# A fused delta-rule and two-MoE kernel: the early groups in an order made step by step from durations, groups 0 and 1 in halves

## Chip, cores and metric

The kernel runs on one core of a Trainium2 chip. The metric is the device time of one execution in microseconds (us), the median of several runs; less is better. Engines are named as in the profile: PE is TensorE, DVE is VectorE, ACT is ScalarE, POOL is GpSimd, SP is SyncE, whose queue issues all loads and stores.

## The reference

A delta-rule attention (4 batches, 8 heads, 768 positions, head size 48) feeds a gated layer of 1536 channels, and that feeds an ELU layer of 2048 channels. Inputs of the attention are float32, the weights of both layers float64.

```python
k_n = k / (np.linalg.norm(k, axis=-1, keepdims=True) + 1e-06)
for t in range(S):
    y[:, :, t] = einsum('bhd,bhde->bhe', q[:, :, t], state)
    v_old = einsum('bhde,bhd->bhe', state, k_n[:, :, t])
    state = state + beta_t * einsum('bhd,bhe->bhde', k_n[:, :, t], v[:, :, t] - v_old)
x = y.transpose(0, 2, 1, 3).reshape(3072, 384)
g = x @ w_gate
x = (g / (1 + exp(-g)) * (x @ w_val)) @ w_out          # first layer, d_ff 1536
h = x @ w_in
out = where(h > 0, h, exp(minimum(h, 0)) - 1) @ w_out2 # second layer, d_ff 2048
```

## The kernel before

**Groups.** The 3072 tokens are 12 groups of 256: two batches by 128 positions each. A group's attention is in the chunked form of the delta rule and has two parts. The first part needs no other group: the norm of k (`norm`, `nkn`), transposes of q and k (`trans`, L207), Gram products (`gram`, L217, masked on DVE at L220), and the inverse of a triangular matrix, done on DVE in some 116 small multiplies and adds between transposes (`inversion`, L234 to L270), copied at L200 to `zt`. The second part is serial from group to group: the x-step (L288: the inverse by v and k, which stand side by side in `R`), four g-steps (L304, copied on ACT at L308, added on DVE at L309), four state rounds `chain` (L322, added at L326), `yall` (L335, copied at L341), and `xtr` (L351), which transposes y into the pair xh, xl (a rounded value on ACT, the remainder by a subtraction on DVE, L356 and L359).

**First layer.** Each group has 12 slices of 128 channels. For each, a gate/value product `gv_pe` (18 matmuls, L478) goes into one of two PSUM tiles gv0, gv1; silu on ACT (L504), multiply on DVE (L505), cast and subtract to hb; and an output product `out1` (9 matmuls, L521) adds into the PSUM tile `acc`, two products behind (`LAG`). After the twelfth slice `acc` is copied by ACT (L528) to `y` and stored to the DRAM tile `x2d`.

**Weights.** They come as the bits of float64 in 18 tiles w0 to w17 (three for two slices) and are decoded by six pieces each: "low" (ACT, L400), "sign" (ACT, L435; in the second layer "and", DVE, L420), "abs" (ACT, L407), "or" (DVE, L425), "cast" (ACT, L440), "sub" (DVE, L444). The weights of the second layer take the places of those of the first as they come free. The second layer (`h2`, `out2`) works on 512 tokens at a time; `load_x2` reads x back from `x2d` before it (L545).

**Order.** A scheduler of the language puts instructions on the engines in the order in which they are written, unless ready earlier; `inorder` forbids it to move those on DVE, ACT and POOL. The start is written out in order by hand: `merge` takes lists of (weight, step) and mixes them in proportion to the weights. Group 0's products stand in one merged, ordered list with the decoding slots and the attention of group 1; from group 1 on the attention of group g+1 is merged with the products of group g (`ATT`), and from g above 1 the last part of the inversion of g+2 is carried into the next period (`XTR`). SP's loads stand where the code issues them: v of group 0 behind w0 and w1.

## Time and profile before

| | |
|---|---|
| median of 3 runs | 1242.88 us (1241.53 to 1244.37) |
| the profiled execution | 1240.22 us, of which the span of the trace is 1238.5 us |
| PE busy | 1148.1 us, 93% of the span |
| DVE busy | 789.2 us, 64% |
| ACT busy | 626.9 us, 51% |
| POOL busy | 67.4 us, 5% |
| chain that ended last | PE 79%, DVE 12%, ACT 5%, issue 2%, DMA 1% |

The shares are over the whole span. The page's row of 40 slices (31 us each) shows PE at 2, 4, 7, 4 tenths in the first four slices and at 9 from the fifth to the last; DVE and ACT are busiest in the first four. The granted clock of PE is under full in slices 2 to 7 and full after. So a reader looks at the first slices apart from the rest.

### The profile page before, as it was taken

The page shows a single profiled execution, that of the slowest core. Times are in us where ns is not written, and L with a number is a line of the kernel's source. Part 1 is how long each engine was busy: PE and PEld are TensorE (multiplying, and loading weights), DVE is VectorE, ACT ScalarE, POOL GpSimd, SP SyncE. Part 2 cuts the span into 40 slices and gives each one's busy share as a digit, 9 for nine tenths or more (in the row PEclk, how much of TensorE's full clock was granted, in tenths as well). Part 3 has the DMA queues.
Part 4 walks back from the last instruction along what each step waited for, and adds up shares of the span by engine and source line. Part 5 has one row for each costly group of instructions (what it writes and reads, how often), then busy time and mean ns, then how long its engine had stood idle before and what let it go on. Part 6 is the DMA issues. An engine that isn't in the chain of part 4 may idle for free.

```text
span 1238.5 us, 31273 instructions
## 1 busy us (share of the span) xinstructions
PE 1148.1 (93%) x13086; PEld 1069.0 (86%) x13086; DVE 789.2 (64%) x2731; ACT 626.9 (51%) x1189; POOL 67.4 (5%) x76
## 2 busy tenths in 40 slices
PE   2474998999999999999999999999999999999998
PEld 2464898889899899999989999989899899899897
DVE  6779648768585849586858664549844545454443
ACT  6597634352526262635344433559744545454443
POOL 4000101010101010100000000000000000000000
PEclk9866799799999999999999999999999999999999
DMA  9730020212121110303030100580000101010000
GB/s 291 197 78 1 14 38 4 41 28 28 27 28 39 16 40 15 53 2 53 2 53 2 29 15 2 181 296 26 21 31 1 52 1 51 1 35 1 26 1 26
DMA packets 106813, 57.15 MB, mean 46 GB/s; under 512 B 76944, under 2 KB 101520, under 8 KB 106672
## 3 DMA queue, kind: packets, MB, share of 16 engines
q1 hardware_dynamic: 106672, 55.16, 17.6%
q8 instruction: 102, 1.67, 0.6%
q14 instruction: 39, 0.32, 0.1%
HBM read 45.71 MB, written 9.44 MB: 45 GB/s over the span
## 4 chain that ended last, share of the span: by engine, by line
PE 79%; DVE 12%; ACT 5%; issue 2%; DMA 1%; POOL 1%; SPq 0%; ACTq 0%; DVEq 0%
PE gv L478 21%; PE acc L521 10%; PE acc L573 8%; PE at L573 8%; PE gv L556 8%; PE at L556 8%; PE at L304 5%; PE at L288 3%; DVE z L262 3%; DVE ain L255 3%; PE at L322 3%; PE at L207 2%; PE at L335 1%; PE at L217 1%; DVE tb L505 1%
## 5 line engine op out<-in xcount | busy, mean ns | idle before, releaser
L478 PE MATMUL gv<-xh,w 128*128 128x256 f32 x1728 | 292.9, 292 | 27.8 <-DVE tb L505 23.4
L478 PEld LDWEIGHTS gv<-xh,w 128*128 128x128 f32 x1728 | 243.6, 196 | 34.7 <-DVE tb L505 25.0
L521 PE MATMUL acc<-hb,w 128*128 128x256 f32 x1296 | 187.4, 290 | 2.0 <-ACT y L528 1.6
L521 PEld LDWEIGHTS acc<-hb,w 128*128 128x128 f32 x1296 | 167.7, 194 | 5.8 <-ACT y L528 1.8
L478 PE MATMUL gv<-xl,w 128*128 128x256 f32 x864 | 155.3, 289 | 0.0
L504 ACT ACTIVATE tb<-gv 128x256 f32<-128x256 f32 x144 | 55.2, 384 | 160.7 <-PE gv L478 158.9
L356 ACT CAST hb<-tb 128x256 fp32r<-128x256 f32 x144 | 58.4, 406 | 149.8 <-DVE tb L505 149.6
L505 DVE TENSOR_TENSOR tb<-gv,tb 128x256 f32<-128x256 f32 x144 | 60.5, 421 | 114.9 <-ACT tb L504 114.2
L478 PEld LDWEIGHTS gv<-xl,w 128*128 128x128 f32 x864 | 127.8, 196 | 0.8 <-DVE xl L359 0.2
L255 DVE TENSOR_TENSOR ain<-z,ain 128x60 f32<-128x60 f32 (+32 forms) x696 | 120.3, 205 | 1.6
L262 DVE TENSOR_TENSOR z<-z,ain 128x60 f32<-128x60 f32 (+32 forms) x696 | 119.7, 210 | 1.4
L563 DVE SCALAR_TENSOR_TENSOR hb<-at,hb 128x512 f32<-128x512 f32 x48 | 33.2, 692 | 84.5 <-ACT hb L562 84.5
L563 DVE SCALAR_TENSOR_TENSOR hb<-gv,hb 128x512 f32<-128x512 f32 x48 | 33.2, 691 | 80.6 <-ACT hb L562 80.6
L359 DVE TENSOR_TENSOR hb<-tb,hb 128x256 fp32r<-128x256 f32 x144 | 60.6, 421 | 28.7 <-ACT hb L356 28.3
L304 PE MATMUL at<-gr,R 32*96 32x80 f32 x1472 | 73.0, 270 | 3.3 <-DVE lc L309 2.5
L304 PEld LDWEIGHTS at<-gr,R 32*96 32x96 f32 x1472 | 61.0, 173 | 14.7 <-DVE lc L309 3.0
L560 ACT ACTIVATE hb<-at 128x512 f32<-128x512 f32 x48 | 28.6, 596 | 85.3 <-PE at L556 85.3
L560 ACT ACTIVATE hb<-gv 128x512 f32<-128x512 f32 x48 | 28.6, 596 | 85.0 <-PE gv L556 85.0
L562 ACT ACTIVATE hb<-hb,neg 128x512 f32<-128x512 f32 x96 | 69.4, 723 | 2.8
L288 PE MATMUL at<-R,zt 64*64 64x96 f32 x768 | 42.9, 264 | 29.9 <-ACT zt L200 29.8
L288 PEld LDWEIGHTS at<-R,zt 64*64 64x64 f32 x768 | 39.5, 147 | 32.9 <-ACT zt L200 31.7
L561 ACT ACTIVATE hb<-hb 128x512 f32<-128x512 f32 x96 | 60.7, 632 | 2.6
(193 smaller groups left out, 2120.6 us busy)
## 6 DMA issues: line engine op xcount, KB each, us to landing
w<-in_moe_w_out_dram SPq DMA_DIRECT2D x28, 384.0 KB, 6.0
w<-in_moe_w_in_dram SPq DMA_DIRECT2D x16, 384.0 KB, 5.2
kp<-in_k_dram SPq DMA_DIRECT2D x12, 384.0 KB, 5.5
qp<-in_q_dram SPq DMA_DIRECT2D x12, 384.0 KB, 4.4
w<-in_moe_w_gate_dram SPq DMA_DIRECT2D x12, 384.0 KB, 8.6
w<-in_moe_w_val_dram SPq DMA_DIRECT2D x12, 384.0 KB, 8.6
R<-in_v_dram SPq DMA_DIRECT2D x24, 192.0 KB, 2.9
x2d<-y SPq DMA_DIRECT2D x12, 256.0 KB, 2.1
```

The source lines that it names most:

```text
L255: V.tensor_tensor(out=t, in0=z[:, l:l + 1, x:y].to_broadcast([128, l, y - x]), in1=an[:, l, 0:l].unsqueeze(2).to_broadcast([128, l, y - x] ...
L262: V.tensor_tensor(out=z[:, 0:l, x:y], in0=z[:, 0:l, x:y], in1=t, op=ALU.add)
L288: nc.tensor.matmul(p[r:r + 64, j], lhsT=zt[r:r + 64, 4 * n + j, :], rhs=R[r:r + 64, 4 * n + j, :], start=True, stop=True, skip_group_check ...
L304: nc.tensor.matmul(ps_[c][0:96, s * 80:s * 80 + 80], lhsT=R[t, u, :], rhs=gr[t, u, 0:80], start=True, stop=True, skip_group_check=True)
L478: nc.tensor.matmul(dst, lhsT=wt[:, a_, kk * 128:(kk + 1) * 128], rhs=xx[:, kk, :], start=(n == 0), stop=(n == 3 * KD - 1))
L505: V.tensor_tensor(out=s, in0=p[:, TB:2 * TB], in1=s, op=ALU.mult)
L521: nc.tensor.matmul(o, lhsT=w[:, a_, d * 128:(d + 1) * 128], rhs=hh[:, b_, :], start=(f == 0 and n == 0 and d != 1), stop=(f == F1 - 1 and ...
L556: nc.tensor.matmul(p, lhsT=W[f][:, 0, a_, kk * 128:(kk + 1) * 128], rhs=x2[n][b_][:, kk, :], start=(m == 0), stop=(m == 3 * KD - 1))
L561: A.activation(out=r, in_=r, func=ACTF.Exp, scale=-1.0)
L562: A.activation(out=r, in_=r, func=ACTF.Identity, bias=neg1, scale=1.0)
L563: V.scalar_tensor_tensor(out=r, in0=p, scalar=0.0, in1=r, op0=ALU.max, op1=ALU.add)
L573: nc.tensor.matmul(ob4[t], lhsT=hh[:, b_, t * 128:(t + 1) * 128], rhs=w[:, a_, :], start=(f == 0 and m == 0), stop=(f == F2 - 1 and m == 2))
```

## The change

The steps of attention, first layer and decoding are cut into single operations, each with an engine and a duration written into the code. Up to group 3 (`GL` = 4 groups of products, the second part of the attention of groups 0 to 4, the first part of groups 0 to 4 and 40% of the inversion of group 5) a greedy planner, `schedule`, takes again and again the step that can begin first by these durations, over threads: the serial attention parts (`thread_second`, biased by -0.3), the first parts (`thread_first`), the products on PE and their ACT and DVE work (`threads_moe`), one thread for each temporary of the decoding (`threads_decode`), and the filling of constants. `in_order` now pins PE's order as well. Ten tiles get their sign by "sign" on ACT as before, eight by "and" on DVE. Groups 0 and 1 go in halves of six slices: first halves of 0 and 1, then second halves of 0 and 1, so that the second nine weight tiles are needed later. The sum of a first half is copied out of `acc` and stored to a new DRAM tile `x2e`, and the reload of x before the second layer adds it (L605). From group 4 on the lists are merged by weight as before. The loads of v of group 0 are now issued behind those of the weights.

```diff
+    x2e = dr.tile([2, 128, KD, TB], F32, name="x2e", tag="x2e")
...
+        ends = ((0, FH), (FH - 1, F1 - 1)) if g < 2 else ((0,), (F1 - 1,))
...
-                                 start=(f == 0 and n == 0 and d != 1), stop=(f == F1 - 1 and n == 2),
+                                 start=(f in ends[0] and n == 0 and d != 1),
+                                 stop=(f in ends[1] and n == 2),
...
+    def out1_copy(g, f):
+        dst = x2d if f == F1 - 1 else x2e
...
+            if n == 0:
+                t2 = TT("z", [128, TB2])
+                for j in range(2):
+                    nc.sync.dma_start(out=t2[:, j * TB:(j + 1) * TB], in_=x2e[j, :, d, :])
+                V.tensor_tensor(out=t, in0=t, in1=t2, op=ALU.add)
...
+    def in_order(x, engines):
+        with ExitStack() as es:
+            for e in engines:
+                if e in last:
+                    es.enter_context(tc.issue_after(last[e]))
...
+    def schedule(threads):
...
+                if not all(a in done for a in s['after']):
+                    continue
+                b = max([s['at'], busy[s['eng']], 0.0 if s['loose'] else
+                         ends[t][0] + (LATENCY if ends[t][1] != s['eng'] else 0.0)] +
+                        [done[a] for a in s['after']])
...
+                if best is None or b + s['bias'] < best[0]:
+                    best = b + s['bias'], t, b, s
...
+            in_order(lambda: s['fn'](*args), list(EN.values()))
...
+        s('SP', 0.0, lambda: (load_v(g, 0), load_v(g, 1)), after=p, loose=True)
...
+        if g == GL + 1:
+            k = int(len(inv) * CUT0)
+            rest.extend((10.0 / len(inv), x) for x in inv[k:])
+            inv = inv[:k] + [None] * 4
...
+            m.append(step('PE', 2.15, lambda b, g=g, f=f: gv_pe(g, f, gvb[b[0]]), name=('pe', g, f),
+                          after=[('xl', g, 0), ('xl', g, 1), ('dec', pair_of(0, f))], take=('gv', 1),
+                          loose=True, bias=0.0))
...
+                l.append(step('ACT', 0.92, lambda d=d: d('low'), at=10.0 + 2.25 * n, **b))
+                if n < NL:
+                    l.append(step('ACT', 1.93, lambda d=d: d('sign'), **b))
+                else:
+                    l.append(step('DVE', 1.03, lambda d=d: d('and'), **b))
...
+        first = thread_first(0)
+        first.insert(4, step('SP', 0.0, lambda: [load_w(n, src1(n)) for n in range(2, NW - 2)],
+                             loose=True))
...
+        seq = [(0, f) for f in fs] + [(1, f) for f in fs] + [(0, FH + f) for f in fs] + \
+            [(1, FH + f) for f in fs] + [(g, f) for g in range(2, GL) for f in range(F1)]
+        z2 = [step('POOL', 8.0, emit_zero2, after=[('kb', 0, 1)], bias=0.2)]
+        schedule([sum([thread_second(g) for g in range(GL + 1)], []),
+                  first + sum([thread_first(g) for g in range(1, GL + 2)], [])] + threads_moe(seq) +
+                 threads_decode() + [z2])
...
+        for g in range(GL, NB):
+            moe = [(0, lambda: load_x2(0))] if g == NB - 1 else []
...
+            run(merge(steps, moe, scale=(0.85, 1.0)))
```

Three places show what moves. The first is SP's queue at the start; `R` receives v, `qp` and `kp` are q and k, `w` are weight tiles. Before:

```order
L160 DMA qp_68<-in_q_dram 128x16x48
L377 DMA w0_2_108<-in_moe_w_gate_dram 128x3x256
L377 DMA w0_2_108<-in_moe_w_val_dram 128x3x256
L377 DMA w1_3_111<-in_moe_w_gate_dram 128x3x256
L377 DMA w1_3_111<-in_moe_w_val_dram 128x3x256
L163 DMA R_69<-in_v_dram 128x8x48 x2
L374 DMA w2_6_141<-in_moe_w_out_dram 128x768 x2
```

After, at the end of the weights:

```order
L410 DMA w13_16_167<-in_moe_w_val_dram 128x3x256
L407 DMA w14_17_170<-in_moe_w_out_dram 128x768 x2
L410 DMA w15_18_173<-in_moe_w_gate_dram 128x3x256
L410 DMA w15_18_173<-in_moe_w_val_dram 128x3x256
L165 DMA R_69<-in_v_dram 128x8x48 x2
L162 DMA qp_68<-in_q_dram 128x16x48
L159 DMA kp_67<-in_k_dram 128x16x48
```

The two loads of v of group 0 moved from behind w1 to behind w15, just ahead of q and k of group 1.

The second is ACT, from the copies of y of group 0 to the copies of its x (`xh`); L400, L435, L407 and L440 are decoding pieces. Before:

```order
L341 COPY y_37_694<-at3_89 128x384
L341 COPY y_37_694<-at0_86 128x384
L440 CAST w6_38_750<-xl1_31_583 128x2x384
L400 ACTIVATE w9_13_162<-w9_13_162 128x768
L435 ACTIVATE w9_13_162<-w9_13_162 128x768
L407 ACTIVATE dt_4_123<-w9_13_162 128x768
L440 CAST w7_39_757<-dt_4_123 128x2x384
L356 CAST xh0_33_653<-at3_89 128x3x128
L356 CAST xh0_33_653<-at0_86 128x3x128
```

After (L214 copies transposes of group 1, L473 is "cast", L440 "abs", L433 "low", L367 the copy of y, L379 that of x):

```order
L214 COPY kq_70<-at2_89 128x4x128
L214 COPY kq_70<-at0_87 128x4x128
L473 CAST w5_33_680<-dt_4_124 128x2x384
L440 ACTIVATE xl1_34_714<-w6_9_146 128x768
L367 COPY y_35_749<-at3_90 128x384
L433 ACTIVATE w7_10_149<-w7_10_149 128x768
L367 COPY y_35_749<-at0_87 128x384
L379 CAST xh0_36_754<-at1_88 128x3x128
L379 CAST xh0_36_754<-at3_90 128x3x128
```

Five pieces of decoding stood between the copies of y and of x; now one does, and copies of group 1 stand ahead of the copies of y.

The third is DVE from the multiply of product 49 (`tb1`), the second of group 4. Before:

```order
L505 TENSOR_TENSOR tb1_181_4863<-gv1_84,tb1_181_4863 128x256
L359 TENSOR_TENSOR hb1_182_4866<-tb1_181_4863,hb1_182_4866 128x256
L309 TENSOR_TENSOR lc_22_423<-at1_87,kq_70 48x4x32
L309 TENSOR_TENSOR lc_22_423<-at2_88,kq_70 48x4x32
L309 TENSOR_TENSOR lc_22_423<-at3_89,kq_70 48x4x32
L309 TENSOR_TENSOR lc_22_423<-at0_86,kq_70 48x4x32
L309 TENSOR_TENSOR lc_22_423<-at1_87,kq_70 48x4x32
L309 TENSOR_TENSOR lc_22_423<-at2_88,kq_70 48x4x32
L309 TENSOR_TENSOR lc_22_423<-at3_89,kq_70 48x4x32
L309 TENSOR_TENSOR lc_22_423<-at0_86,kq_70 48x4x32
L505 TENSOR_TENSOR tb0_184_4949<-gv0_83,tb0_184_4949 128x256
```

After, the end of that stretch, some 60 rows behind the multiply of product 49 (`tb1_182`), up to the multiplies of products 50 and 51 (L278 and L285 are the multiply and add of the inversion of group 5):

```order
L278 TENSOR_TENSOR ain_72<-z_179_4661,ain_72 128x36
L552 TENSOR_TENSOR hb1_183_4830<-tb1_182_4827,hb1_183_4830 128x256
L278 TENSOR_TENSOR ain_72<-z_179_4661,ain_72 128x42
L285 TENSOR_TENSOR z_179_4661<-z_179_4661,ain_72 128x6x6
L542 TENSOR_TENSOR tb0_185_4911<-gv0_84,tb0_185_4911 128x256
L285 TENSOR_TENSOR z_179_4661<-z_179_4661,ain_72 128x6x7
L278 TENSOR_TENSOR ain_72<-z_179_4661,ain_72 128x35
L542 TENSOR_TENSOR tb1_187_4992<-gv1_85,tb1_187_4992 128x256
```

Before, group 5's g-step adds stood there; now its inversion does, and the subtraction that makes hb of product 49 stands behind 60 of its rows.

## Rows read from the trace of the kernel before

**Rows 1.** Stretches: us, PE, PEld, DVE, ACT, POOL busy (instructions), granted clock, DMA, GB/s.
```profile
60.00:90.00 30.00, 20.36 (x282) 17.94 (x282) 22.52 (x41) 27.80 (x34) 2.52 (x2) 0.61 0.34 80
...
210.00:240.00 30.00, 29.32 (x595) 26.15 (x592) 19.70 (x72) 14.68 (x33) 2.18 (x3) 0.77 0.23 42
...
498.00:556.40 58.40, 58.40 (x923) 55.53 (x922) 42.73 (x194) 26.25 (x63) 4.67 (x6) 1.00 0.17 29
```

**Rows 2.** Timeline of DVE: start, us, line, operation, out<-in, count [idle before <-releaser].
```profile
16.43 2.15 DVE L234 STREAM_TRANSPOSE ain<-gr 128x256 f32<-128x256 f32 x4
...
22.39 0.19 DVE L255 TENSOR_TENSOR ain<-z,ain 128x31 f32<-128x31 f32 x1
...
37.93 1.06 DVE L270 STREAM_TRANSPOSE ain<-z 128x512 f32<-128x512 f32 x1
39.02 1.61 DVE L200 COPY zt<-ain 32x512 f32<-32x512 f32 x2
...
78.04 0.55 DVE L359 TENSOR_TENSOR xl<-at,xh 128x384 fp32r<-128x384 f32 x1
...
170.31 1.02 DVE L359 TENSOR_TENSOR xl<-at,xh 128x384 fp32r<-128x384 f32 x2 [3.36 <-ACT xh L356]
...
244.13 1.02 DVE L359 TENSOR_TENSOR xl<-at,xh 128x384 fp32r<-128x384 f32 x2
```

**Rows 3.** Chain of waits, 370 to 445 us: start, us, engine, tile, line, count.
```profile
371.81 2.16 PE gv L478 x18
373.96 1.08 PE acc L521 x9
375.04 2.26 PE gv L478 x18
...
396.55 0.85 PE at L322 x32
...
418.39 1.17 issue
...
440.13 2.79 PE at L288 x64
```

**Rows 4.** Timeline of SP's queue, 0 to 60 us.
```profile
39.38 0.49 SPq L160 DMA_DIRECT2D qp<-in_q_dram  x1
```

**Rows 5.** Loads of q (tile qp), 0 to 80 us, three of them.
```profile
DMA to landing us min/median/max: 5.1/5.4/9.1
```

**Rows 6.** Timeline of PE, 0 to 100 us.
```profile
39.74 5.89 PE L288 MATMUL at<-R,zt 64*64 64x96 f32 x64 [23.91 <-ACT zt L200]
...
90.09 2.73 PE L217 MATMUL at<-kq 48*32 48x64 f32 x128 [5.02 <-ACT kq L200]
```

**Rows 7.** Timeline of ACT around 60 us.
```profile
59.70 1.92 ACT L435 ACTIVATE w<-w 128x768 f16<-128x768 f32 x1
...
62.22 0.81 ACT L440 CAST w<-xh 128x768 fp32r<-128x768 f32 x1
```

**Rows 8.** Groups by line, DVE, 498 to 556.4 us: count | busy, mean ns | idle.
```profile
L505 DVE TENSOR_TENSOR tb<-gv,tb 128x256 f32<-128x256 f32 x13 | 5.5, 421 | 11.2 <-ACT tb L504 11.1
...
L326 DVE TENSOR_TENSOR sv<-at,sv 48x192 f32<-48x192 f32 x8 | 2.8, 352 | 0.2
L309 DVE TENSOR_TENSOR lc<-at,kq 48x128 f32<-48x128 f32 x8 | 2.3, 282 | 1.5 <-ACT lc L308 1.3
...
L188 DVE TENSOR_TENSOR kp<-kp,sm 128x384 f32<-128x384 f32 x2 | 1.1, 554 | 0.0
...
L171 DVE TENSOR_REDUCE sm<-ain 128x16 f32<-128x768 f32 x1 | 1.0, 954 | 0.7 <-POOL ain L170 0.7
...
L177 DVE TENSOR_TENSOR sm<-sm,sm 128x16 f32<-128x16 f32 x1 | 0.2, 176 | 0.0
```

**Rows 9.** Timeline of DVE, 790 to 797 us, decoding pieces "and" and "or".
```profile
792.99 1.03 DVE L420 TENSOR_SCALAR w<-w 128x768 uint8<-128x768 uint8 x1 [0.56 <-ACT w L400]
794.12 0.96 DVE L425 SCALAR_TENSOR_TENSOR gr<-gr,w 128x768 int32<-128x768 int32 x1
```

**Rows 10.** Timeline of PE, 790 to 800 us.
```profile
794.05 1.33 PE L521 MATMUL acc<-hb,w 128*128 128x256 f32 x9 [1.56 <-ACT y L528]
```

More of the change, by code (lines that the diff above doesn't have):

```diff
@@ L63, in delta_moe_kernel @@
     NHB = 3
+    FH = F1 // 2
     NTB = 2
@@ L189, in nkn, with nkn_a @@
                         op=ALU.mult)
-        A.copy(out=R[:, u, 0:D], in_=kk)
+    def nkn_a(g, a):
+        u = slice(a * 8, a * 8 + 8)
+        A.copy(out=R[:, u, 0:D], in_=kp[:, u, 0:D])
     def kb(g, a):
@@ L446, in decode @@
         if steps:
-            return {'low': low, 'sign': sign, 'abs': p0, 'or': p2, 'cast': cast, 'sub': sub}
+            return {'low': low, 'sign': sign, 'and': p1, 'abs': p0, 'or': p2, 'cast': cast, 'sub': sub}
         return [low, p0, p1, p2, p3]
@@ new lines, in delta_moe_kernel, with traced @@
+    last = {}
+    busy = {e: 0.0 for e in EN}
+    busy['SP'] = 0.0
+    done = {}
+    units = {'at': [0.0] * C, 'g0': [0.0] * C, 'gv': [0.0] * len(gvb), 'y': [0.0]}
+    taken = {}
+    def traced():
+        return nc.cur_bb.bb.instructions
+    def in_order(x, engines):
[3 more added lines that the diff above has]
+                    es.enter_context(tc.issue_after(last[e]))
+            n = len(traced())
+            x()
+            for i in traced()[n:]:
+                last[i.engine] = i
@@ new lines, in yall, with xtr, trans, gram @@
+    def yall(g):
+        yalloc()
+        for a in range(2):
+            b = at()
+            yall_pe(g, a, b)
+            yall_out(a, b)
+    def xtr(g, a):
+        b = at()
+        xtr_pe(a, b)
+        xtr_hi(g, a, b)
+        xtr_lo(g, a, b)
+    def trans(a, which):
+        b = at()
+        trans_pe(a, which, b)
+        trans_out(a, which, b, False)
+    def gram():
+        for a in range(2):
+            for par in range(2):
+                b = at()
+                gram_pe(a, par, b)
+                gram_out(a, par, b)
@@ new lines, in merge, with run, pinned, wrap @@
+    def merge(*ls, scale=None):
+        res = []
+        for i, l in enumerate(ls):
+            sc = scale[i] if scale else 1.0
+            tot = sum(w for w, _ in l) or 1.0
+            p = 0.0
+            for w, x in l:
+                res.append(((p + w / 2) / tot * sc, i, len(res), (w, x)))
+                p += w
+        return [x for *_, x in sorted(res, key=lambda y: y[:3])]
+    def run(l):
+        for _, x in l:
+            x()
+    def pinned(l):
+        def wrap(x):
+            def f():
+                with ExitStack() as es:
+                    for e in (EN['DVE'], EN['ACT']):
+                        if e in last:
+                            es.enter_context(tc.issue_after(last[e]))
+                    x()
+            return f
+        return [(w, wrap(x)) for w, x in l]
@@ L686, in delta_moe_kernel @@
+    NM = 9
+    NL = 10
+    GL = 4
+    LC = 2
+    COLD = 1.8
     CUT = 40
+    CUT0 = 0.4
+    rest = []
     LAG = 2
@@ L759, in emit_all @@
         buf['dt'] = TT("dt", [128, 2, 2, DM], I32)
-        tmps = ("xh1", 0, "xl1", 1)
-        dec = {}
-        def step(n, what):
-            if n not in dec:
-                dec[n] = decode(n, tmps, True)
-            dec[n][what]()
-        def slot(k):
-            l = []
-            for n, ws in ((k + 2, ('low', 'sign', 'abs')), (k + 1, ('or',)), (k, ('cast',)),
-                          (k - 1, ('sub',))):
-                for w in ws:
-                    if 0 <= n < NW and (n >= NL or w not in ('low', 'sign')) and (n > 1 or w != 'abs'):
-                        l.append((0.9 if w in ('or', 'sub') else 0.2, lambda n=n, w=w: step(n, w)))
-            return l
@@ L777, in emit_all @@
-        run(inorder([norm_]))
-        for n in range(2, NW - 2):
-            load_w(n, src1(n))
-        run(inorder([tq, (0, lambda: step(0, 'low')), tk, gm, (0, emit_zero2)]))
-        early = [(1, lambda n=n, w=w: step(n, w)) for n in range(NL) for w in ('low', 'sign', 'abs')
-                 if (n, w) != (0, 'low') and (w != 'abs' or n < 2)]
-        inv = inversion(0)
-        run(inorder(merge([(0.1, x) for x in inv[:-4]], early)))
-        load_q(1)
-        body, tail = attention(0, 1)
@@ new lines, in emit_all @@
+        for e in ('POOL', 'ACT', 'DVE'):
+            busy[e] = 4.0
+        fs = list(range(FH))
+        seq = [(0, f) for f in fs] + [(1, f) for f in fs] + [(0, FH + f) for f in fs] + \
[4 more added lines that the diff above has]
+                 threads_decode() + [z2])
@@ L801, in emit_all @@
+        held = seq[-LAG:]
         late = []
```

589 lines of the change are left out of this document (379 added, 210 removed).

## The prediction

> **What bounds the kernel now.** I read the page first, then the table of stretches, then the chain of waits, then each engine's rows where the chain leaves TensorE (PE). Over the whole span PE looks full (the table of busy times above), but that is an average over several regimes. In a settled group, 58.4 us long, PE is busy without a gap while VectorE (DVE) has 42.7 us and ScalarE (ACT) 26.3 us of work; early on, PE has 20 us of work in 30 at a granted clock of 0.61, and there ACT has 27.8 [rows 1]. The reader is to see two parts: from about 330 us to the end the time is PE's own work, and of what comes before, only what moves the start of that part counts. I follow that by steps. An "x" is the pair of tiles xh, xl that a group's gate/value products read; the last subtraction that makes it ends at 78.6 for group 0, 171.3 for group 1 and 245.2 for group 2 [rows 2]. Gate/value product number 48, the first of group 4, starts at 375.0, and the x-step of group 6 at 440.1 [rows 3]. From that x-step on both kernels run the same code, and the order of the instructions is the same but for the reload of x ahead of the second half, so the rest, 1238.5 - 440.1 = 798.4 us, is a constant, and I predict when that x-step starts.
>
> **Step 1, to x of group 0: 78.6 becomes 77.2.** Two things pull against each other. The loads of v of group 0 now stand on SP behind all 32 weight loads instead of behind four (the first place shown). At that place of the queue, the q of group 1 was issued at 39.4 before [rows 4] and took 9.1 us to land, the longest of three [rows 5]: 48.5. v goes out one load ahead of it, so I take 46.5 as landing. The first x-step reads v; it ran at 39.7 [rows 6], when its other input, the inverse, was just there. So +6.8. Bounds: 0 if the load is there in time, +9 if it lands like q. Against it, ACT: between the first copy of the g-step and the second copy of x there stand 20 pieces of weight decoding before and 9 after (the second place shown is the end of this stretch), and ACT is full there [rows 1]. A sign piece and the abs piece behind it take 2.5 from 59.70 to 62.22, and a cast 0.8 [rows 7]. The eleven that go are 2 signs, 1 low and 4 abs (2 pairs at 2.5, 3 alone at 0.85) and 4 casts of 0.75, 10.5; two copies of group 1 that are put in take back 1.2: -9.3. The square root of group 1 also stands there and waits for group 1's k, which comes late behind the weights; I put +1.1 for that. 78.6 + 6.8 - 9.3 + 1.1 = 77.2.
>
> **Step 2, to the end of group 1's inversion: 106.5.** DVE's row of work is nearly bare now. From 77.2: two copies of k 1.0, Gram products 2.7 at the low clock [rows 6], four masks 1.7, at 0.42 like a product's multiply [rows 8], four transposes 2.15, the inversion 15.5 (22.39 to 37.93, with nothing between), back-transpose 1.06 [rows 2], five products' multiply and subtract at 0.42 each, 4.2 [rows 8], one decode subtract 0.95: 29.3.
>
> **Step 3, to x of group 1: 171.3 becomes 143.** Busy DVE in order: 13 "or" and "sub" pieces at 0.96 and 3 "and" pieces at 1.03, 15 [rows 9]; norm and scaling 0.95 + 1.1 + six small ones of some 0.2, 3.3; 16 adds of 0.28, 4.5; 12 of the 16 state adds of 0.35, 4.2; one product and x 1.9 [rows 8]: 29, less 2 that overlap in the x-step. On top come waits that nothing covers: copies of the inverse 1.6 [rows 2], the x-step 4 (5.9 cold, 2.8 warm [rows 3, 6]), one product of 2.16 and three state rounds of 0.85, half covered [rows 3]: 9.5. 106.5 + 36.5 = 143. By the order PE has 6 products ahead of that x, where before it had 11; the halves let it be so: product 6 onward is group 1's first half and uses the same nine decoded tiles.
>
> **Step 4, to x of group 2: 245.2 becomes 220.** Before took 73.9 us from x to x with no decoding left in it. After carries tiles 12 to 17 here: 5 "or", 5 "sub" and 3 "and", 12.6 us on DVE [rows 9], and their ACT pieces. I take half of it as hidden (bounds none and all): +6.3; and -3 because product and inversion pieces now stand in the order of their times. 143 + 77 = 220. Products 15, 16 and 17 each need a tile that is decoded here, so PE stands idle some 15 us of the last 44.
>
> **Step 5, to product 48: 375.0 becomes 357.** Now PE is the bound. 28 products of 2.16 and 30 output products of 1.08 [rows 3] are 92.9; two groups of attention at 58.4 - 12 x 3.24 = 19.5 are 39; the four state rounds of group 4 find no filler left, at 1.17 each [rows 3], 5. 220 + 137 = 357. Here the halves pay: 18 us ahead.
>
> **Step 6, to the x-step of group 6: 440.1 becomes 432.** This gives back more than half. At product 48 the old kernel has nearly all of group 5's inversion behind it; the new one has hardly begun it, so it and the one of group 6 fall in one period; the third place shown has inversion pieces, on DVE, where eight adds stood. DVE, with a whole second front: 42.7 [rows 1] plus 1.7 + 2.15 + 15.5 + 1.06 = 63.1. DVE also waits with nothing to put in: Gram 1.9 and x-step 2.8 on PE, copies 1.6, the first g-step 1.3 [rows 2, 3, 8], three state rounds 2.6, the norm of group 6 about 1.3: 11.5. 357 + 75 = 432; PE's 58.4 of work there fits under it. The bound on the other side is PE's own 58.4: 415.
>
> **Step 7, the partial sums: +2.** The halves store two partial outputs and read them back at the reload of x before the second half: six loads into one buffer and three adds more in SP's and DVE's order. In the reload of before, PE stood 1.56 us behind a copy out of PSUM on ACT [rows 10]. After, that copy stands ahead of the third reload, -1.6; the load and the decoding of the first second-half weight behind it come 1.4 to 2.1 later, and waiting for the one buffer adds up to 4. Bounds -1.6 and +6; I take +2. The extra copies out of PSUM on ACT hide behind a product of 2.16.
>
> **Sum.** 440.1 - 432 = 8 gained, 2 lost: 6 us. The profiled execution took 1240.2 us, its span 1238.5; it stands 2.7 below the median of the runs, 1242.9. 1240.2 - 6 = 1234; by the median 1237.
>
> **Rivals.**
> First, a larger gain, 1225. v lands before the inverse is done (-6.8) and decoding costs step 4 nothing (-6): 1237 - 12. For it: v is half the bytes of a q, and the DMA engines have little to do behind the weights. Against it: q's 9.1 us at that place. The Trainium skill (DMA: Bandwidth & Descriptors, Queues, rings and completion order) says that on each engine the descriptors of a queue are consumed in ring order; by that v cannot overtake the weights, which leaves this rival its second half only. Nothing in the trace of before shows v in that place. Chance 0.25.
>
> Second, slower, 1249. In steps 3 and 4 PE waits every few us, and its clock sits at the low level, 1.2 GHz. For it: 60 to 90 us at 0.61, and even 210 to 240, PE nearly full, at 0.77 [rows 1]. The second part of step 4 holds 30 us of PE's work in 44; the clock decides once the mean grant there is under 30/44 = 0.68, and at 0.54 it makes 56 us of 44: +12. Against it: 1.00 in the settled group. The Trainium skill (TensorE: Matmul & The Clock Gate, HAM oscillation) says the same of a kernel that waits again and again: each burst starts cold. By that rule alone step 4 ends near 232 and the time is 1249. Chance 0.25.
>
> Third, no change, 1243. The gain of step 5 goes back whole: step 6 takes 81 instead of 75, because DVE's order, merged by weights and not by times, makes PE and DVE wait for each other in turn. Chance 0.12. The forecast has 0.38.
>
> **How the numbers follow.** A measurement of this kernel can tell about 0.2%, 2.5 us. The forecast's own range is 1230 to 1244: of its 0.38, 0.30 faster, 0.06 same, 0.02 slower. The first rival is 0.25 faster; the second 0.23 slower, 0.02 same; the third 0.10 same, 0.02 slower. Faster 0.55, same 0.18, slower 0.27. Low end: the first rival and 3 us more from step 6 nearer to its other bound, 1222; high end: the second rival with 3 more at step 7, 1252.
>
> **What would show it.** Right: the first x-step starts near 46.5 and waits for a DMA; x of group 0 near 77; x of group 2 near 220 with PE idle between products 15 and 17; product 48 near 357; 74 to 76 us from there to the x-step of group 6, with PE idle before output product 49. Wrong: a first x-step at 40 (first rival), a granted clock under 0.68 between 175 and 220 (second), a stretch of over 80 us behind product 48 (third), or a reload of x that holds PE for over 6 us.

## The result and the profile after

The changed kernel takes 1233.49 us, the median of five runs (1227.81 to 1234.04), against 1242.88 us before. The ratio of the runs' times is 0.9913 (95% interval 0.989 to 0.9937), 0.9% faster; the two medians alone give 0.992. The forecast was 1237. The profiled execution has a span of 1229.5 us, 9.0 less than that of before.

The page of the changed kernel: busy time by engine, the granted clock in 40 slices, and the shares of the chain that ended last.

```profile
PE 1142.2 (93%) x13086; PEld 1060.3 (86%) x13086; DVE 800.9 (65%) x2742; ACT 615.4 (50%) x1185; POOL 69.9 (6%) x76
...
PEclk9987889999977999999999999999999999999999
...
PE 77%; DVE 12%; DMA 4%; ACT 4%; issue 2%; SPq 1%; POOL 0%; DVEq 0%; ACTq 0%; POOLq 0%
```

The page tells little: PE's share is 93% as before. One sees a granted clock under 0.9 in slices 3 to 6 and, new, again in the twelfth and thirteenth, from about 340 to 400 us. (Before, that row still has a 7 in the eighth slice, so the clock was not full right behind the seventh.) What happened is read from a table of the prediction's steps. All times are starts or ends in us, worked out from the timelines of DVE and PE; "x" is the end of the last subtraction that makes a group's x. Differences are taken before rounding.

| step | before | predicted | after |
|---|---|---|---|
| first x-step starts | 39.7 | 46.5 | 44.7 |
| x of group 0 | 78.6 | 77.2 | 72.8 |
| end of inversion of group 1 | 125.7 | 106.5 | 100.6 |
| x of group 1 | 171.3 | 143 | 134.4 |
| x of group 2 | 245.1 | 220 | 210.1 |
| product 47 starts | 371.6 | | 326.3 |
| Gram products of group 5 end | 347.9 | | 347.0 |
| product 48 starts | 374.9 | 357 | 342.0 |
| x-step of group 6 starts | 440.1 | 432 | 425.6 |
| product 62 starts | 449.1 | 441 | 438.7 |
| product 134, ahead of the reload | 789.5 | 781 | 779.3 |
| product 143, behind it | 823.7 | 818 | 814.8 |

(Where the prediction names no time for a step, the column is empty or takes the old distance from the step before, with the 2 us of step 7 in the last row.) The lead grows to 45 us at product 47, and 33 of these are there at product 48, 14.4 at the x-step of group 6, 10.4 at product 62 and 8.9 at product 143, the last of the first layer. So most of what the first stretch won was given back in one place, between 326 and 439 us. Two things are easily overlooked. Only two of the 18 matmuls of product 48 run at 342.0; the other 16 come from 346.9 on, behind the last state rounds and the Gram products of group 5, so the lead there is nearer to 28. And these Gram products, with which the inversion of group 5 can begin, end only 1 us earlier than before, while product 47 starts 45 us earlier:

```profile
346.20 1.73 PE L217 MATMUL at<-kq 48*32 48x64 f32 x128
```

This is the kernel before; the row of the changed kernel, 346.62, stands in the chain below. Products had run ahead, attention's first part had not.

The table of stretches says where PE's time went: first before (to x of group 0, 1, 2, to product 48, to product 62, and all of it), then after, between the same steps. The first bound lies 1.4 us behind x of group 0 before and 3.2 after, and the matmuls between two bounds are not the same ones, since products have moved; those of the last row are. The columns are those of [rows 1].

```profile
0.00:80.00 80.00, 36.24 (x624) 31.52 (x625) 56.27 (x200) 56.15 (x73) 16.87 (x23) 0.82 0.78 214
80.00:171.30 91.30, 66.93 (x871) 63.25 (x870) 63.85 (x218) 58.89 (x94) 7.72 (x7) 0.76 0.06 10
171.30:245.00 73.70, 68.96 (x1053) 64.70 (x1053) 51.97 (x247) 29.69 (x67) 5.22 (x6) 0.91 0.20 34
245.00:375.00 130.00, 124.88 (x1877) 118.91 (x1877) 95.57 (x461) 53.46 (x127) 9.68 (x11) 0.97 0.15 26
375.00:449.10 74.10, 71.16 (x1105) 67.18 (x1104) 49.84 (x213) 37.71 (x88) 6.94 (x7) 1.00 0.13 24
0.00:449.10 449.10, 368.17 (x5522) 345.56 (x5522) 317.51 (x1335) 235.90 (x447) 46.44 (x53) 0.90 0.25 57
```

```profile
0.00:76.00 76.00, 32.64 (x738) 28.36 (x742) 57.13 (x207) 48.32 (x70) 19.82 (x25) 0.91 0.76 206
76.00:134.40 58.40, 43.29 (x621) 39.36 (x614) 51.31 (x192) 37.92 (x67) 5.96 (x5) 0.77 0.11 19
134.40:210.00 75.60, 68.14 (x960) 64.25 (x960) 58.73 (x210) 40.20 (x82) 5.55 (x5) 0.93 0.20 49
210.00:342.00 132.00, 129.69 (x1980) 123.42 (x1979) 90.44 (x397) 58.96 (x139) 9.86 (x10) 1.00 0.14 29
342.00:438.70 96.70, 87.04 (x1241) 81.41 (x1237) 70.55 (x341) 39.01 (x89) 7.73 (x8) 0.84 0.13 22
0.00:438.70 438.70, 360.81 (x5522) 336.79 (x5522) 328.16 (x1343) 224.41 (x443) 48.92 (x53) 0.91 0.25 60
```

Up to product 62 both kernels run the same 5522 matmuls. PE is busy 368.2 us with them before and 360.8 after, and it idles 80.9 and 77.9 us. Of the 10.4 us, then, 7.4 are busy time, fewer us for the same matmuls, and only 3.0 are idle time. The mean granted clock of 0.91 for 0.90 says little on it, since it counts idle time too: in the first 76 us it is 0.91 here and 0.66 in the run of experiment 2, with 738 matmuls and the same busy time (32.6 and 32.9 us). By lines, most of the 7.4 stand in the g-steps, up to product 62 (before, then after):

```profile
L304 PE MATMUL at<-gr,R 32*96 32x80 f32 x768 | 42.0, 283 | 3.1 <-DVE lc L309 2.3 <-DVE dt L309 0.5 <-ACT R L200 0.3
L322 PE MATMUL at<-gr,R 32*96 32x80 f32 x768 | 35.8, 279 | 7.9 <-DVE lc L332 6.5 <-DVE w L332 1.2
```

With the 64 matmuls that write other tiles it is 46.9 and 41.1 us, 5.8 less. Such a row is not a matter of the clock alone: before the change, at a granted clock of 1.00, the 32 matmuls of one g-step took 1.77 us at 383 and 0.92 at 390.

By stretch the idle time is 43.8, 24.4, 4.7, 5.1 and 2.9 before and 43.4, 15.1, 7.5, 2.3 and 9.7 after: 9.7 us won up to x of group 1 and 6.7 lost again in the last stretch, where the granted clock also falls from 1.00 to 0.84.

The loss begins where the planner's part ends. The chain of waits of the changed kernel from there to product 61 (start, us, engine, tile, line, count):

```profile
342.09 0.44 PE gv L511 x2
...
343.14 1.65 PE at L233 x114
344.79 1.83 issue
346.62 0.37 PE at L233 x2
346.99 6.64 PE gv L511 x34
...
369.22 1.15 DVE ain L293
370.45 0.43 ACT zt L214
...
373.17 2.78 PE at L310 x56
...
377.11 2.07 PE at L322 x23
...
379.49 2.29 PE at L322 x32
...
382.30 2.30 PE at L322 x31
...
389.19 3.61 PE at L221 x16
...
427.35 4.50 PE at L310 x62
431.85 2.36 PE gv L511 x18
```

And three stretches of it:

```profile
358.00:371.00 13.00, 8.14 (x54) 7.94 (x53) 12.62 (x80) 2.13 (x5) 0.49 (x1) 0.74 0.01 2
371.00:380.00 9.00, 8.74 (x127) 7.63 (x127) 5.31 (x15) 7.33 (x16) 2.02 (x2) 0.98 0.00 0
380.00:390.00 10.00, 10.00 (x122) 8.71 (x118) 4.62 (x16) 4.68 (x13) 1.65 (x2) 0.50 0.22 41
```

The Gram products of group 5 (L233) end at 347; only then can its inversion begin, and DVE is full with it until 370 (12.62 of 13 us). PE still has products of group 4 to run, since their x is there from 342 on, but it stops in the middle of an output product. Here is the wait on PE, then the instruction on DVE that ends it:

```profile
365.43 1.01 PE L568 MATMUL acc<-hb,w 128*128 128x256 f32 x3 [4.86 <-DVE hb L552]
```

```profile
364.95 0.42 DVE L552 TENSOR_TENSOR hb<-tb,hb 128x256 fp32r<-128x256 f32 x1
```

This is the subtraction of product 49 that stands in DVE's order behind 60 rows of the inversion (the third place of the change). These 4.86 us are half of the 9.7 that PE idles in the stretch; most of the rest is waiting for the copies of the two inverses (2.4) and 1.8 ahead of the last Gram products. The x-step (L310) and the first g-steps (L322) follow at a granted clock of 0.98; then PE is busy all 10 us of 380 to 390, but at 0.50, the low level, 1.2 GHz. After the second inversion 62 of the 64 matmuls of the x-step of group 6 take 4.50 us, at a mean grant of 0.62, where the x-step took 2.79 before [rows 3] at 1.00.

### The profile page after: what moved, and what is told of

It is laid out like the page before. It is cut to its first block, busy times and chain, and to the rows that moved or that the text cites. A ratio compares the mean times of both kernels' runs of the same rounds, so it can differ in the third digit from the quotient of the medians.

```text
span 1229.5 us, 31347 instructions
## 1 busy us (share of the span) xinstructions
PE 1142.2 (93%) x13086; PEld 1060.3 (86%) x13086; DVE 800.9 (65%) x2742; ACT 615.4 (50%) x1185; POOL 69.9 (6%) x76
## 4 chain that ended last, share of the span: by engine, by line
PE 77%; DVE 12%; DMA 4%; ACT 4%; issue 2%; SPq 1%; POOL 0%; DVEq 0%; ACTq 0%; POOLq 0%
PE gv L511 21%; PE acc L568 10%; PE acc L633 8%; PE at L633 8%; PE at L616 7%; PE gv L616 7%; PE at L322 4%; PE at L344 3%; PE at L310 3%; DVE z L285 2%; DVE ain L278 2%; DMA w<-in_moe_w_val_dram 2%; PE at L221 2%; PE at L358 1%; PE at L233 1%
## 5 line engine op out<-in xcount | busy, mean ns | idle before, releaser
L542 DVE TENSOR_TENSOR tb<-gv,tb 128x256 f32<-128x256 f32 x144 | 60.5, 421 | 105.2 <-ACT tb L538 104.4
L285 DVE TENSOR_TENSOR z<-z,ain 128x60 f32<-128x60 f32 (+32 forms) x696 | 119.5, 210 | 1.4
L278 DVE TENSOR_TENSOR ain<-z,ain 128x60 f32<-128x60 f32 (+32 forms) x696 | 119.3, 205 | 1.5
L310 PE MATMUL at<-R,zt 64*64 64x96 f32 x768 | 41.6, 265 | 42.2 <-DMA R<-in_v_dram 29.8
L552 DVE TENSOR_TENSOR hb<-tb,hb 128x256 fp32r<-128x256 f32 x144 | 63.3, 440 | 23.9 <-ACT hb L548 23.4
L310 PEld LDWEIGHTS at<-R,zt 64*64 64x64 f32 x768 | 38.5, 149 | 44.8 <-ACT w L468 30.0
L322 PE MATMUL at<-gr,R 32*96 32x80 f32 x1472 | 66.9, 267 | 8.1 <-DVE lc L332 6.7
L322 PEld LDWEIGHTS at<-gr,R 32*96 32x96 f32 x1472 | 55.7, 171 | 18.7 <-DVE lc L332 4.8
```

Source lines behind the costliest of these rows:

```text
L278: V.tensor_tensor(out=t, in0=z[:, l:l + 1, x:y].to_broadcast([128, l, y - x]), in1=an[:, l, 0:l].unsqueeze(2).to_broadcast([128, l, y - x] ...
L285: V.tensor_tensor(out=z[:, 0:l, x:y], in0=z[:, 0:l, x:y], in1=t, op=ALU.add)
L310: nc.tensor.matmul(p[r:r + 64, j], lhsT=zt[r:r + 64, 4 * n + j, :], rhs=R[r:r + 64, 4 * n + j, :], start=True, stop=True, skip_group_check ...
L322: nc.tensor.matmul(banks[c][0:96, s * 80:s * 80 + 80], lhsT=R[t, u, :], rhs=gr[t, u, 0:80], start=True, stop=True, skip_group_check=True)
L552: V.tensor_tensor(out=hh[:, 1, :], in0=gvp.pop((g, f))[1], in1=hh[:, 0, :].bitcast(F32), op=ALU.subtract)
```

## Experiments

The theory with which they began: the changed kernel loses at this joint because its products ran ahead of attention. The rival for each is in its expectation. Each run was timed in five rounds beside the kernel before, whose median was 1241.0 to 1242.4 there; all ratios are against that kernel, and the changed kernel's is 0.9913 (0.989 to 0.9937). Where two runs are compared, it is by their ratios, 0.001 being 1.2 us, and by the spans of their traces; the medians of different rounds are not subtracted.

**1. v early.** The term of step 1 by itself: v of group 0 back behind w1.

```diff
             load_w(n, src1(n))
+        load_v(0, 0)
+        load_v(0, 1)
...
-        s('SP', 0.0, lambda: (load_v(g, 0), load_v(g, 1)), after=p, loose=True)
+        if g:
+            s('SP', 0.0, lambda: (load_v(g, 0), load_v(g, 1)), after=p, loose=True)
```

> The changed kernel with the two loads of v of group 0 issued behind w1 again, as before the change; all else as it is. In the changed kernel the first x-step starts at 44.7 and its releaser is the load of v; the inverse is transposed back by 40.3. Theory of step 1 (v late costs 6.8 us of x of group 0): the first x-step starts at 42, x of group 0 is ready at 70 instead of 72.8, and since the planner's order is the same everything behind moves by the same 2.7: 1231. Rival (ACT's decoding sets x of group 0, not v): x of group 0 stays at 72.8 and the time at 1233.5.

1232.55 us, 0.9911 (0.9887 to 0.9936): no difference. The first x-step is earlier, x of group 0 stays at 72.8, as the rival said, but not for the rival's reason. PE's timeline of the changed kernel and then of this run:

```profile
44.74 1.55 PE L310 MATMUL at<-R,zt 64*64 64x96 f32 x15 [29.76 <-DMA R<-in_v_dram]
```

```profile
41.17 2.18 PE L310 MATMUL at<-R,zt 64*64 64x96 f32 x18 [26.11 <-ACT zt L214]
```

The chain of waits of the changed kernel and then of this run, towards x of group 0:

```profile
43.89 5.91 DMA kp<-in_k_dram
49.87 0.09 issue
49.96 1.48 POOL ain L170
51.46 0.95 DVE sm L173
52.41 1.73 DVE w L477 x2
...
54.93 0.29 DVE lc L332
```

```profile
40.01 10.29 DMA kp<-in_k_dram
...
50.46 1.48 POOL ain L170
```

k of group 1 lands at about 50 in both, behind the weights; its norm (L170, L173) stands in DVE's fixed order ahead of the first g-step adds of group 0 (L332). So DVE waits for k of the next group, and whatever v costs before 50 us is covered by that wait.

**2. No halves.** The planner, with the new place of v and the new signs, but without the halves.

```diff
-        ends = ((0, FH), (FH - 1, F1 - 1)) if g < 2 else ((0,), (F1 - 1,))
+        ends = (0,), (F1 - 1,)
...
-        seq = [(0, f) for f in fs] + [(1, f) for f in fs] + [(0, FH + f) for f in fs] + \
-            [(1, FH + f) for f in fs] + [(g, f) for g in range(2, GL) for f in range(F1)]
+        seq = [(g, f) for g in range(GL) for f in range(F1)]
```

> The changed kernel without halves: groups 0 and 1 run their twelve slices in one piece, no partial sums are stored or added; the planner and its durations stay. Theory (the halves make the lead at product 48, because product 6 onward need not wait for tiles 9 to 17): products 6 to 11 wait for decoding, product 48 starts near 355 instead of 342.0, the reload of x is 1.3 us shorter, and the time is 1240 to 1245. Rival (the lead comes from the planner's durations, the halves only move decoding): product 48 near 342 and 1231 to 1233.

1235.1 us, 0.9948 (0.9929 to 0.9967). Product 48 starts at 359.5, 17.5 us later, as the theory said; but the x-step of group 6 is only 4.2 later (429.9) and the time 0.35%, some 4 us. Neither expectation fits: the halves do make the lead at product 48, and three quarters of that lead are worth nothing. The change without them makes 0.5%. Its interval and that of the changed kernel overlap a little, so the 4 us rest on the trace too, where product 62 is 4.2 later.

**3. The inversion of group 5 planned to its end.**

```diff
-    CUT0 = 0.4
+    CUT0 = 0.965
```

> The changed kernel with 0.965 instead of 0.4 of the inversion of group 5 in the planner's part, so that only its back-transposition and copies are merged by weight. Theory (the stretch from product 48 to the x-step of group 6, 83.6 us, is long because the planner's products are used up by 326 while x of group 4 is ready at 342.2; DVE begins that inversion at 349.8 in any case): the same time, 1231 to 1236. Rival (the merged order costs it: the subtraction of product 49 stands behind 60 rows of the inversion): with the weights of the inversion out of the merge, products 49 to 51 come through, the stretch is 75 us and the time 1225.

1231.15 us, 0.9913 (0.9894 to 0.9931): the same, as the theory said. Where the planner's list ends does not matter, since DVE starts that inversion at 350 in any case. The rival's shorter stretch does not come: from product 48 to the x-step of group 6 it takes 84.1 us, and PE still waits 4.8 us for a subtraction that makes hb.

**4. Attention first, everywhere.**

```diff
-        e = -0.3 if g == 0 else 0
+        e = -0.3 if g == 0 else -0.2
...
-            l.append(step(*x, bias=-0.3, **k))
+            l.append(step(*x, bias=-1.0, **k))
```

> The changed kernel with other biases in the planner alone: the serial attention parts at -1.0 instead of -0.3, the first parts of groups 1 to 5 at -0.2 instead of 0. By the order of instructions the x-step of group 4 then stands at product 28 instead of 45 and that of group 5 at product 50 instead of 53. Theory (products run ahead of attention and are missing as filler later): product 48 starts near 345, the x-step of group 6 comes 58 to 65 us later, 403 to 412, and the time is 1210 to 1220. Rival (attention ahead takes PE's filler from the early stretches, where DVE and ACT decode; PE stands idle there instead): product 48 later than 355 and the time 1233 or more.

1260.7 us, 1.0153 (1.0134 to 1.0172): slower, and the theory as put failed; the rival's sign came, product 48 at 390.8. The products' work on DVE has a bias of -0.1; with -0.2 the inversion goes ahead of it, and each stands in DVE's order as one block of 122 pieces. What follows is read from the stretch between 213 and 300 us, where the changed kernel's PE is nearly full and this run's is busy 52.6 of 87 us. In 33.7 of its 34.4 idle us PE's products wait for the multiply on DVE (L542) that reads a product's PSUM tile; the longest of the two waits is 18.4 us:

```profile
213.00:300.00 87.00, 52.60 (x964) 48.96 (x963) 61.15 (x312) 28.59 (x64) 5.60 (x6) 0.80 0.17 34
```

**5. Attention first, but not the pieces of the inversion.**

```diff
-            l.append(step(*x, bias=e, **k))
+            l.append(step(*x, bias=e if g < 2 else dict(PE=-2, ACT=-0.3, DVE=0).get(x[0], 0), **k))
...
-            l.append(step(*x, bias=-0.3, **k))
+            l.append(step(*x, bias=-0.3 if g < 2 else -2, **k))
...
-    CUT0 = 0.4
+    CUT0 = 0.965
```

> The changed kernel with other biases in the planner for groups 1 to 5: the serial attention steps at -2.0 instead of -0.3, PE's steps of the first parts at -2.0 and ACT's at -0.3 instead of 0, the pieces of the inversion at 0 as before, so that they still give way to the products' work on DVE (in the slower run with biases -1.0 and -0.2 each inversion stood on DVE as one block of 122 pieces); 0.965 of the inversion of group 5 in the planner's part. By the order of instructions the x-step of group 4 stands at product 39 instead of 45, that of group 5 at 49 instead of 53. Theory (the changed kernel loses at the joint because products ran ahead of attention): product 48 starts at 340 to 350, the x-step of group 6 58 to 65 us later, PE has no idle stretch of over 5 us there, and the time is 1215 to 1225. Rival (attention's chain, not the mixture, sets the x-step of group 6, and it is no shorter this way): x-step of group 6 at 420 to 430 and 1228 to 1236.

The expectation misstates the edit: the diff shows that the biases hold from group 2 on, not from group 1. 1234.18 us, 0.9932 (0.9908 to 0.9957): no difference from the changed kernel. Product 48 comes at 361.9, the x-step of group 6 at 430.7, 68.8 us behind it, and product 62 at 439.7 (438.7 in the changed kernel). PE idles 4.5 us in the last stretch instead of 9.7, but 10.9 instead of 7.5 from x of group 1 to x of group 2 and 6.2 instead of 2.3 up to product 48. So the rival's numbers came, within 1 us. The joint was eased, and the groups ahead of it paid.

**6. The joint in the order of its list.**

```diff
-            run(merge(steps, moe, scale=(0.85, 1.0)))
+            l = merge(steps, moe, scale=(0.85, 1.0))
+            if g == GL:
+                l = [(w, lambda x=x: in_order(x, [EN['DVE'], EN['ACT'], EN['POOL']])) for w, x in l]
+            run(l)
```

> The changed kernel with the merged period of group 4's products held in the order of its list on DVE, ACT and POOL, as the start was before the change. On DVE the inversion of group 5 then stands ahead of the multiply of product 49. Theory (the x-step of group 5 waits for that inversion, which starts when the Gram products are done; the order beside it is of no account): the time stays within 4 us of 1233. Rival (what the merged order loses is the waiting of DVE and PE for each other): 1224 or less if the list's order is the better one, 1240 or more if it is the worse one.

1237.5 us, 0.9958 (0.9938 to 0.9979), 5.6 us above the changed kernel by the ratios, 4.4 by the spans. The x-step of group 5 starts at 371.9, as in the changed kernel (371.7), so the order beside the inversion does not move it; the x-step of group 6 comes at 434.9 instead of 425.6. That is just outside the theory's bound of 4 us and short of the rival's 1240: the order is of some account behind the x-step of group 5, and the list's own is not the better one. From 342 to 430 PE waits 10.7 us for the multiplies of products on DVE (L542), and no longer for hb.

**7. No read-back of the partial sums.**

```diff
-            if n == 0:
-                t2 = TT("z", [128, TB2])
-                for j in range(2):
-                    nc.sync.dma_start(out=t2[:, j * TB:(j + 1) * TB], in_=x2e[j, :, d, :])
-                V.tensor_tensor(out=t, in0=t, in1=t2, op=ALU.add)
```

> The changed kernel without reading the partial sums of groups 0 and 1 back: the six loads and three adds at the reload of x are left out, so the output lacks the first halves of groups 0 and 1. By the trace the lead of the changed kernel shrinks from 10.2 to 8.9 us at the reload. Theory of step 7 (the read-back costs +2): 1231 to 1232.5. Rival (it is hidden and the shrinkage is another wait): 1233 to 1234.

1232.91 us, 0.9919 (0.9891 to 0.9946): no difference. From product 134 to 143 it takes 35.5 us with the read-back and without it (34.2 before the change). The waits of PE at the reload lie at other places (idle time in brackets), here in the changed kernel and then in this run:

```profile
781.92 1.34 PE L568 MATMUL acc<-hb,w 128*128 128x256 f32 x9 [0.32 <-ACT y L583]
```

```profile
786.50 1.33 PE L568 MATMUL acc<-hb,w 128*128 128x256 f32 x9 [1.91 <-ACT y L583]
```

The copy that held PE for 1.56 us before [rows 10] holds it for 0.32 after and for 1.91 without the read-back. So the read-back costs nothing that shows in the time. What the 1.3 us are stays open: PE idles 2.9 us in the stretch with the read-back, 4.0 without it and 4.1 before the change, so no wait of PE accounts for them.

**8. Half of an inversion left out.**

```diff
-            rest.extend((10.0 / len(inv), x) for x in inv[k:])
+            part = inv[k + 50:]
+            rest.extend((10.0 / len(inv) * (len(inv) - k) / len(part), x) for x in part)
```

> The changed kernel with 50 of some 120 pieces of the inversion of group 5 left out, all in the merged part (the output of group 5 is wrong by it); about 12 us of DVE's row of dependent pieces between product 48 and the x-step of group 5. Theory (attention's chain sets the x-steps of groups 5 and 6 and with them the end): x-step of group 5 at 360 instead of 371.7, x-step of group 6 at 415 instead of 425.6, the time 1222 to 1226. Rival (product 48 and PE's work behind it set the end): product 48 at 342, x-step of group 6 within 3 us of 425, the time 1231 or more.

1221.4 us, 0.9836 (0.9809 to 0.9864): some 10 us less than the changed kernel (9.6 by the ratios, 9.8 by the spans). In the trace the x-step of group 5 starts at 351.4, 20.4 earlier, that of group 6 at 420.5, 5.2 earlier, and that of group 7 at 478.3, 9.3 earlier. The theory is confirmed for the end, and product 48, at 343.0, has no part in it. (With fewer pieces in the list the x-step also stands four products earlier in PE's order, at 49.) The way is not quite the one foretold: half of the gain appears only with the x-step of group 6, which runs between products 60 and 61: product 61 follows product 60 by 6.1 us, as before the change, and not by 10.4.

**9. Attention first from group 3 on.**

```diff
-            l.append(step(*x, bias=e, **k))
+            l.append(step(*x, bias=e if g < 3 else dict(PE=-2, ACT=-2, DVE=0).get(x[0], 0), **k))
...
-            l.append(step(*x, bias=-0.3, **k))
+            l.append(step(*x, bias=-0.3 if g < 3 else -2, **k))
...
-    CUT0 = 0.4
+    CUT0 = 0.965
```

> The run with PE's priority changed only for groups 3 to 5: there the serial attention steps and the first parts on PE and ACT stand at -2.0, the inversion's pieces at 0; 0.965 of the inversion of group 5 in the planner's part. Up to x of group 2 the order is that of the changed kernel (in the run that changed it from group 1 on, PE's idle time between 137 and 208 us grew by 3.4 us and that between 208 and 362 by 3.9, while the joint lost 5 less). By the order the inversion of group 5 ends at product 47 and its x-step stands at 49. Theory (idle time of PE only moves: what the joint gains, the stretch in front of it pays, since attention's steps wait on each other there): 1230 to 1235. Rival (the loss of that run came from its early part, and the joint's gain is real): 1226 to 1229.

(The run that it compares itself with is experiment 5, whose priority began at group 2.) 1223.67 us, 0.9861 (0.9839 to 0.9882): the rival is right, with 6.5 us less than the changed kernel by the ratios and 6.2 by the spans, where it had said 4.5 to 7.5. The Gram products of group 5 end at 328.7 instead of 347.0. Product 48 comes at 357.9, 15.8 later than in the changed kernel, and yet the x-step of group 6 is 3.7 earlier and product 62 7.8. The stretches of this run, to be laid beside the last two of the changed kernel:

```profile
210.00:342.00 132.00, 124.99 (x2006) 118.43 (x2006) 97.64 (x444) 55.82 (x129) 9.96 (x10) 0.92 0.13 26
342.00:438.70 96.70, 93.21 (x1342) 89.10 (x1341) 68.32 (x308) 46.34 (x111) 8.88 (x9) 1.00 0.13 25
```

In the last one PE is busy 93.2 us at a clock of 1.00 instead of 87.0 at 0.84 and gets 101 matmuls more done; the stretch in front gives 4.7 us of idle time for it and a clock of 0.92. The gap at the joint was a loss that could be recovered. This run differs from experiment 5 in the group from which the priority holds and in ACT's bias, so which of the two makes the 9 us between them is not told apart.

**10. The planner's part two groups longer.**

```diff
-    GL = 4
+    GL = 6
```

> The changed kernel with the planner's part two groups longer (products of groups 0 to 5 instead of 0 to 3); the joint to the merged part comes two groups later. By the order, x-steps stand at the same products up to group 4, the next at 58 and 70. Theory (the joint costs some 20 us of the lead once, wherever it stands, and the planner's part holds PE full before it): within 3 us of 1233. Rival (products run further ahead with each planned group, so the joint loses more): 1237 or more. Other rival (the merged periods themselves are the slower ones): 1229 or less.

1236.86 us, 0.9967 (0.9953 to 0.9982): slower than the changed kernel by some 0.5%. The median falls between the theory's bound and the first rival's and is nearer to the rival: product 62 has run ahead to 414.5 (438.7 in the changed kernel), and product 134 comes 2.7 us later than there, so more is lost behind the later joint.

**11. All signs on ACT.**

```diff
-    NL = 10
+    NL = 18
```

> The changed kernel with the sign of all 18 tiles on ACT as before the change, none by the and piece on DVE: eight pieces of 1.03 us less on DVE, eight of 1.9 more on ACT, from about 100 us on. Theory (between x of group 0 and x of group 2 DVE's row of pieces sets the time, ACT has room): x of group 2 up to 4 us earlier, the time 1229 to 1233. Rival (ACT sets it there: 37.9 us of work in the 58.4 before x of group 1): x of group 2 later by up to 10 us, the time 1234 to 1238.

1228.21 us, 0.9893 (0.987 to 0.9915). x of group 2 comes at 208.6, 1.5 us earlier, as the theory said; the intervals of this and the changed kernel overlap, so the gain in time is unclear.

**12. Experiments 9 and 11 together.** To the edits of experiment 9 this one:

```diff
-    NL = 10
+    NL = 18
```

> The run with attention's priority on PE for groups 3 to 5 (1223.7) and all signs on ACT (1228.2 for that alone, against 1233.5 of the changed kernel) together. If the two gains stand in different stretches and add up (x of group 2 earlier by 1 to 4 us, the joint closed): 1217 to 1221. If the first stretch's gain is swallowed by the planned groups behind it: 1222 to 1225.

1222.3 us, 0.9843 (0.9824 to 0.9863), the fastest kernel that computes everything; against experiment 9 (0.9861) the intervals overlap, so the second expectation holds: the signs add little or nothing. Against the changed kernel it is 8.7 us by the ratios and 8.2 by the spans.

## Why the prediction was right, and where its steps were not

The time, the sign and the range held, and so did the outline: a lead from the halves, more than half of it given back where two inversions meet. That the time is right to 3.5 us is luck in part, since the steps lead to it by errors of up to 15 us that offset each other.

- **Step 1.** 72.8 instead of 77.2. The load of v behind the weights behaved as priced (44.7 for 46.5, with the DMA as releaser: the two loads land at 44.6 and 45.4, behind the last weight at 44.0, so the first rival's half on v did not come), but the +6.8 did not reach x: k of group 1, for which I had put +1.1, is what DVE waits for, and it covers v (experiment 1). That wait should have been the term; I had added v's delay to x as if nothing else stood in between. In effect the copies of the first g-step begin 5.0 us later than before (52.6 for 47.5), and from there to x it takes 20.2 us instead of 31.0; the term of -9.3 for ACT's decoding is in line with that, though no run changed it by itself.
- **Steps 2 and 3.** From x of group 0 to the end of the inversion 27.8 us for 29.3, and to x of group 1 33.7 for 36.5. DVE's row of work, counted piece by piece, was the right view. Two of the sums in step 3 do not come out as written: the 13 and 3 decoding pieces make 15.6, not 15, and the waits, with the state rounds half covered, 9.0, not 9.5; the two nearly cancel.
- **Step 4.** 75.8 for 77. The idle time in it was 7.5 us and not 15. The second rival's condition did not arise: between 175 and 220 us the granted clock is 0.89, over the 0.68 at which it decides.
- **Step 5.** 131.9 for 137. PE is the bound, as said, with 2.3 us of idle time; the 5 us for the last state rounds seem not lost, but only because product 48 begins between them with two matmuls. Counted to its third matmul, at 346.9, the step takes 136.8.
- **Step 6 is the step that failed.** I let the stretch start at product 48 and put 75 us behind it; it takes 83.6 (78.7 from the third matmul of product 48), and product 48 does not set its end: in experiment 2 product 48 is 17.5 us later and the x-step of group 6 only 4.2, and in experiment 9 product 48 is 15.8 later and the x-step 3.7 earlier. What sets it is attention's own row from the Gram products of group 5 at 347 on, 1 us earlier than before the change, and two inversions one behind the other on DVE (experiment 8, with half of one inversion, is 10 us faster); that nothing else sets it is not shown, since the order beside the inversions counts too (experiment 6). I had both inversions, but hung them on the wrong start. Of the third rival the sign came true (over 80 us behind product 48, counted from its first matmul), not its price, since the lead at product 48 was 15 us larger than forecast.
- **The rest is not a constant.** I took the same order of instructions from the x-step of group 6 on for the same time. That x-step stood in readiness before, 5 us behind its inverse, and came just in time after: PE waited, and it ran at the low clock for the most part (4.50 us for 2.79). 4.0 us of the lead went there.
- **Step 7.** +1.3 in the trace, +2 forecast, but the cause named is not it: without the read-back the stretch is as long (experiment 7).

Added up: x of group 2 was 9.9 earlier than forecast and product 48 15.0, and 8.6 in step 6 and 4.0 behind it took most of that back; step 7 was 0.8 cheaper, and 0.2 went between products 62 and 134. That gives 15.0 - 8.6 - 4.0 + 0.8 - 0.2 = 3.0 us under the forecast, and the median is 3.5 under it. The halves, which the prediction credits with the lead, make only some 4 of the 11 us that the ratio gives.

The forecast of what would be seen was right in the DMA ahead of the first x-step and in PE's idle time before output product 49, where PE waits 4.86 us. It was wrong in PE standing idle between products 15 and 17 for 15 us, in the times of x of groups 0 and 2 and of product 48, which came 4, 10 and 15 us earlier, and in the 74 to 76 us from product 48 to the x-step of group 6.

## What to carry to other kernels

A lead of one kind of work is worth nothing where two kinds must meet again: 45 us of products ahead became 10, because the serial work had hardly moved (the Gram products of group 5 end at 347.0 instead of 347.9) and the products still to run had to share DVE with its long row. A greedy order takes whatever is ready; give the serial thread priority on the engine where it is short (PE), but leave its long row of small pieces behind the short work that frees buffers, or the row blocks the engine (1260.7 us against 1223.7). And follow the serial chain through a joint, not a count of the filler.

## What was not expected of the hardware

The granted clock was low while PE showed no idle time. From 358 to 371 us PE was busy for 8.14 of 13 us; then for 8.74 of 9, at a granted clock of 0.98; and then without a gap for the 10 us from 380 to 390, at 0.50, its low level. That does not mean that the same work takes half as long at the full clock. In the chain of waits 23 matmuls of the g-steps take 2.07 us ahead of the fall, and 32 and 31 of them take 2.29 and 2.30 behind it, so these small matmuls were held by something else at either level; what that is stays open. The x-step of group 6 is the clearer case: 4.50 us at a mean grant of 0.62 for 2.79 at 1.00.

And with the same 5522 matmuls PE is busy 7.4 us less after the change: most of what it gained is not the idle time in which the prediction counted. Of the 7.4 us, 5.8 stand in the g-steps. How much of them is the clock and how much a closer row of matmuls was not told apart.
